# Early access to the gate and up weights, and another order of the first two slabs, in a GFNet and GEGLU kernel

## The chip, the cores and the metric

One NeuronCore of a Trainium2 chip runs the whole kernel. The metric is the time of one execution in microseconds (us) on the device, as the median over runs. Five engines work side by side, each in the order of its own queue: TensorE (PE; its weight loads are shown as PEld), VectorE (DVE), ScalarE (ACT), GpSimd (POOL) and SyncE (SP). They wait for each other through semaphores. 16 DMA engines move data between HBM and the on-chip memory; before the change, all transfers of this kernel are issued by SP.

## The reference

```python
x = A_x                                        # (1, 2048, 640), bfloat16
xn = _layernorm(x, axis=-1)                    # over the 640 columns, eps 1e-5
X = jnp.fft.rfft2(xn.astype(jnp.float32), axes=(-2, -1))
s = irfft2(X * (w_r + 1j * w_i), s=(2048, 640))             # bfloat16
g = silu((gelu(xn @ w_gate) * (xn @ w_up)) @ w_down)        # gelu: tanh form, F = 1536
return x + s * g
```

Two branches start from the same normalized rows: a filter in the frequency domain, and a feed-forward block (FFN) with a gate. Their product is added to the input.

## The kernel before, in words

The 2048 rows are cut into 16 slabs of 128 rows (`X[:, n1, :]`), four slabs to a group. All matmuls, those of the Fourier transforms too, run on TensorE, and the program writes out the order of every engine's queue by hand: a list `back` holds the steps of the FFN (pieces of gate and up for a group, then the down projection), and a table `plan` hangs the other work (statistics, norms, transposes, folds, transforms) on the steps by number, through `put(step, function, arguments)`. For each step the FFN work is issued first and then what `plan` holds for it.

The change lies in the start, up to about 18 us. There:

- `load_x(n0, n)` (L85) and `load_w(k, t0, t1)` (L89) issue the loads on SP: slabs of x, and tiles `t0` to `t1` (128 columns each, for all 640 rows) of the gate (`k = 0`, `Wg`) or up weights (`k = 1`, `Wu`). `load_gu` loads both. Their order is that of the source lines.
- `half_stats(n1, k)` (L183) is the bn_stats instruction of one half of a slab's columns on VectorE; with `k = 1` it is followed by the aggregate (L188), which gives mean and variance (`mva`). `stats` does both halves.
- `root(n0, n)` adds eps on VectorE (`ve`, L197) and raises to the power of -0.5 on GpSimd (`rst`, L199). `norm` (L205) subtracts the mean and multiplies by the root on VectorE; `norm_parts` does it for columns 0 to 383 and 384 to 639 in turn.
- `slab_Tparts(n1)` (L849, L850) transposes a slab on TensorE into a PSUM tile in the same two parts (chunks 0 to 2 and 3 to 4 of 128 columns) and copies each to `xnT`. For slab 0 both copies are ScalarE's; for slab 1 the first is ScalarE's and the second VectorE's. `slab_T` (L531 to L535) does a whole slab.
- `ffn_slab(j, tk)` computes for slab `j` alone, 128 rows wide, the pieces `(t, k)` in `tk`; tiles 0 to 2 are done so for slabs 0 and 1. A piece is five matmuls (L789) into a PSUM bank, two banks for gate (`psg`) and two for up (`psu`). ScalarE then applies gelu to a gate piece (`ge`, L793), and VectorE multiplies the up piece by it into `uT` (L795). `ffn_part(0, t, h)` does the remaining tiles of group 0 for two slabs at a time (256 columns wide), first tiles 3 to 7 of slabs 0 and 1, then tiles 0 to 7 of slabs 2 and 3, which need their norm and transposes.
- `warm_pe(n)` (L590) issues `n` matmuls of 256 columns on a tile of ones, whose results nobody reads.
- `inv_consts` and `inv_rest` compute fourteen columns of constants on VectorE (one element per partition) for the tables of the inverse transform, which `ft_v(5)` and later steps (L353, ScalarE) read. `vt_iota` and `lists` are index ramps on GpSimd.
- ScalarE loads a table of functions when the function to come is not in the one that is loaded (ACT_TABLE_LOAD). The first activation, `warm`, brings gelu's table ahead of its use.

The start as it is issued: loads; constants; statistics and root of slab 0; 19 warming matmuls; norm of slab 0; statistics of slab 1; transposes and copies of slab 0; two warming matmuls; root of slab 1; then the steps of `back`.

Of the kernel before, what the change touches and what calls it, by code (L numbers as in the profile page):

```python
# [10 lines left out]
BF16 = mybir.dt.bfloat16  # L11
# [3 lines left out]
P = 128  # L15
# [62 lines left out]
def build(nc, env):  # L78
# [5 lines left out]
    def load_x(n0, n, eng=nc.sync):  # L84
        eng.dma_start(out=X[:, n0:n0 + n, :], in_=xv[:, n0:n0 + n, :])  # L85

    def load_w(k, t0, t1):
        f0, f1 = t0 * P, t1 * P
        nc.sync.dma_start(out=(Wg, Wu)[k][:, :, f0:f1], in_=(wgv, wuv)[k][:, :, f0:f1])  # L89

    def load_gu(t0, t1):
        for k in range(2):
            load_w(k, t0, t1)

    load_x(0, 1)
    load_w(0, 0, 3)
    load_x(1, 1)
    load_w(1, 0, 1)
    load_w(1, 1, 3)
    load_x(2, 2)  # L100
    load_gu(3, 5)
    load_gu(5, 7)
# [87 lines left out]
    def stats(n1):  # L190
        for k in range(2):
            half_stats(n1, k)

    def root(n0, n):
        m = mva[n0 // 4][:, n0 % 4:n0 % 4 + n, :]
        ve = work.tile([P, 4], FP32, tag="ve", name="ve")[:, 0:n]
        nc.vector.tensor_scalar(out=ve, in0=m[:, :, 1], scalar1=1e-5, scalar2=None, op0=ALU.add)  # L197
        r = work.tile([P, 4], FP32, tag="rst", bufs=4, name="rst")[:, 0:n]
        nc.gpsimd.tensor_tensor(out=r, in0=ve, in1=mhalf[:, 0:n], op=ALU.pow)  # L199
        rall[n0] = r  # L200
        for k in range(n):
            rstd[n0 + k] = r[:, k:k + 1]

    def norm(n1, c0=0, c1_=D):
        nc.vector.tensor_scalar(out=X[:, n1, c0:c1_], in0=X[:, n1, c0:c1_], scalar1=mva[n1 // 4][:, n1 % 4, 0:1],  # L205
                                scalar2=rstd[n1], op0=ALU.subtract, op1=ALU.mult)
        if c1_ == D:
            done.add(("n", n1))
# [3 lines left out]
    negpi = c1("negpi")  # L212
    nc.vector.memset(negpi, -PI_SAFE)
    warm = c1("warm")
    nc.scalar.activation(out=warm, in_=negpi, func=ACT.Gelu_apprx_tanh)
    b_0, b_1 = c1("b_0"), c1("b_1")
    nc.vector.memset(b_0, 320.0)
    nc.vector.memset(b_1, 0.0)
# [99 lines left out]
    fwd_consts()  # L318
    vt_iota(0)
    stats(0)  # L320
    root(0, 1)
    inv_consts()

    def tinv_phase(h):
        sl = slice(8 * h, 8 * h + 8)
# [502 lines left out]
        for t, k in tk:  # L828
            ffn_piece(0, t, k, j * P, j * P + P)

    GG, REST = ((0, 0), (1, 0)), ((0, 1), (2, 0))

    def run(*items):
        for it in items:
# [8 lines left out]
    def slab_Tparts(n1):  # L843
        if n1 == 0:
            xnT[0] = xg.tile([P, 5, 512], BF16, tag="xg", name="xnT0")
        for (a, b), ev in zip(PARTS, (nc.scalar.copy, nc.scalar.copy if n1 == 0 else nc.vector.tensor_copy)):
            pt = psB.tile([P, 5, P], BF16, tag="b")
            for c in range(a, b):
                nc.tensor.transpose(out=pt[:, c, :], in_=X[:, n1, c * P:(c + 1) * P], identity=ident)  # L849
            ev(out=xnT[0][:, a:b, n1 * P:n1 * P + P], in_=pt[:, a:b, :])  # L850
        done.add(("T", n1))

    NP = 8
    back = [(run, (ffn_slab, 0, GG), (norm_parts, 1), (vt_iota, 1), (ffn_slab, 0, REST), (slab_Tparts, 1),
             (ffn_slab, 0, ((1, 1), (2, 1))),
             (half_stats, 2, 0)),
            (run, (ffn_slab, 1, GG + REST[:1]), (half_stats, 2, 1), (root, 2, 1), (ffn_slab, 1, REST[1:])),
            (run, (ffn_slab, 1, ((1, 1), (2, 1))), (norm, 2), (stats, 3), (root, 3, 1))]
    for h in range(2):
        for t in range(0 if h else 3, NP):  # L860
            back.append((ffn_part, 0, t, h))
# [9 lines left out]
    def put(s, *item):  # L871
        plan[s].append(item)

    put(5, norm, 3)
    put(5, slab_T, 2, 1)
    put(6, slab_T, 3, 0)
    for g in range(5):
        put(3 + g, ft_v, g)
        put(8 + g, ft_v, 5 + g)
# [91 lines left out]
            if (n0 + k) % 2 and 1 < (n0 + k + 3) // 2 < 8:  # L971
                put(min(d + (5 + k if n == 3 else 2), vs0 + 41), load_xt, (n0 + k + 3) // 2)

    warm_pe(19)
    norm_parts(0)
    stats(1)
    slab_Tparts(0)
    warm_pe(2)
    root(1, 1)
    inv_rest()  # L980

    put(5, phase_const)

# [35 lines left out]
```

## Time and profile before

| what | us |
|---|---|
| median of 3 runs (lowest, highest) | 201.75 (201.51, 202.1) |
| the profiled execution, its own time | 201.22 |
| its span, first to last instruction | 199.4 |
| TensorE busy | 193.1 (97% of the span) |
| VectorE, ScalarE, GpSimd busy | 131.6, 123.1, 38.0 |
| slab 0 lands (issue 0.72, 2.3 to landing) | 3.05 |
| slab 1 lands (issue 1.65, 3.7 to landing) | 5.35 |
| norm of slab 0, of slab 1 starts | 5.09, 7.63 |
| slab 0's first FFN matmul | 6.59 |
| slab 1's first FFN matmul | 9.01 |

The profile is that of one execution. Times in it count from the start of its span. A line of the timeline gives start, duration, engine, source line, operation, what is written from what, and in brackets how long the engine was idle before it and what ended that. A line of a stretch gives its ends and length, then for TensorE, its weight loads, VectorE, ScalarE and GpSimd the busy time with the number of instructions, then the granted TensorE clock, the DMA engines' share and GB/s. The chain of waits is followed back from the last instruction; each piece has its start, its length and what it is.

### The profile page before, as it was taken

What the parts mean: (1) busy time and instruction counts of PE and PEld (TensorE: products, weight loads), DVE (VectorE), ACT (ScalarE), POOL (GpSimd) and SP (SyncE); (2) the same over time, 40 slices, a digit from 0 to 9 for tenths busy, and PEclk for the clock granted to TensorE, in tenths of its full rate; (3) what the DMA queues carried; (4) which work ended last, traced back from release to release, by engine and by line L of the source; (5) the groups of instructions that cost most, each with busy time, mean ns of one, the idle gap of its engine ahead of it and who ended that gap; (6) DMA issues with size and microseconds to landing.
All of it is one profiled execution on the core that took longest, in us unless ns stands there. A gap on an engine that the chain in (4) does not pass through costs nothing.

```text
span 199.4 us, 4150 instructions
## 1 busy us (share of the span) xinstructions
PE 193.1 (97%) x1534; PEld 118.9 (60%) x1549; DVE 131.6 (66%) x320; ACT 123.1 (62%) x217; POOL 38.0 (19%) x62
## 2 busy tenths in 40 slices
PE   7989999999999999999999999999999999999993
PEld 5778854777555555576633333457765555556772
DVE  7876869999899832223666556423339786878673
ACT  2547657956976677634788687523474747376632
POOL 5427769999030000000000000000000000000000
PEclk9999999999999999999999999999999999999999
DMA  5999999464566647329962022359800416142522
GB/s 176 333 327 337 388 308 186 88 210 173 154 150 158 150 126 278 104 66 298 282 182 98 5 99 102 132 135 292 235 0 35 135 36 194 36 131 46 187 69 66
DMA packets 40325, 32.44 MB, mean 163 GB/s; under 512 B 15088, under 2 KB 38256, under 8 KB 40048
## 3 DMA queue, kind: packets, MB, share of 16 engines
q1 hardware_dynamic: 40304, 32.17, 55.3%
q8 instruction: 12, 0.20, 0.4%
q14 instruction: 9, 0.07, 0.1%
HBM read 19.03 MB, written 7.88 MB: 135 GB/s over the span
## 4 chain that ended last, share of the span: by engine, by line
PE 91%; DVE 4%; DMA 1%; issue 1%; ACT 1%; POOL 1%
PE psu L789 25%; PE psg L789 25%; PE psg L814 13%; PE psu L814 13%; PE pv L706 2%; PE pd L553 2%; PE pu L653 2%; PE pz L543 2%; PE pd L574 2%; PE px L626 2%; DVE st L183 1%; DMA X<-in_A_x_dram 1%; PE pd L557 1%; POOL rst L199 1%; DVE X L205 1%
## 5 line engine op out<-in xcount | busy, mean ns | idle before, releaser
L789 PE MATMUL psu<-xnT,Wu 128*128 128x512 bf16 (+2 forms) x288 | 60.8, 339 | 0.9 <-DVE uT L795 0.3
L789 PE MATMUL psg<-xnT,Wg 128*128 128x512 bf16 (+2 forms) x287 | 60.5, 338 | 0.5 <-issue 0.2
L795 DVE TENSOR_TENSOR uT<-psu,ge 128x512 bf16<-128x512 f32 (+2 forms) x59 | 34.4, 586 | 27.2 <-PE psu L789 21.0
L814 PEld LDWEIGHTS <-uT 128*128 128x128 bf16 x396 | 37.3, 98 | 14.0 <-issue 0.4
L793 ACT ACTIVATE ge<-psg 128x512 bf16<-128x512 f32 (+2 forms) x59 | 30.6, 519 | 22.9 <-PE psg L789 21.1
L789 PEld LDWEIGHTS <-Wu 128*128 128x128 bf16 x295 | 26.9, 98 | 24.7 <-issue 3.2
L789 PEld LDWEIGHTS <-Wg 128*128 128x128 bf16 x295 | 26.6, 98 | 20.6 <-issue 1.6
L814 PE MATMUL psg<-Wd,uT 128*128 128x320 bf16 (+1 forms) x204 | 30.7, 294 | 0.0
L814 PE MATMUL psu<-Wd,uT 128*128 128x320 bf16 (+1 forms) x192 | 28.7, 296 | 0.0
L638 DVE TENSOR_TENSOR X<-xs,W 128x972 bf16<-128x972 bf16 (+2 forms) x22 | 13.3, 648 | 10.2 <-ACT xs L634 9.2
L579 ACT CAST zd<-pd 128x660 bf16<-128x660 f32 x16 | 11.3, 709 | 9.8 <-PE pd L576 6.1
L708 ACT CAST W<-pv 128x640 bf16<-128x640 f32 x16 | 11.1, 696 | 5.0 <-PE pv L706 5.0
L183 DVE BATCH_NORM_STATS2 st<-X 128x6 f32<-128x320 bf16 x32 | 14.0, 477 | 0.3 <-DMA X<-in_A_x_dram 0.3
L731 ACT ACTIVATE W<-pd 128x960 bf16<-128x960 f32 (+2 forms) x14 | 10.1, 780 | 5.6 <-PE pd L557 5.5
L659 ACT CAST X<-pu 128x486 bf16<-128x486 f32 (+4 forms) x22 | 12.3, 558 | 0.3
L634 ACT CAST xs<-px 128x972 bf16<-128x972 f32 (+2 forms) x11 | 10.3, 938 | 2.9 <-PE px L626 2.9
L545 ACT CAST GEN<-pz 128x640 bf16<-128x640 f32 x16 | 11.2, 700 | 1.2 <-PE pz L543 1.2
L823 DVE SCALAR_TENSOR_TENSOR G<-th,psg 128x320 bf16<-128x320 f32 x8 | 3.9, 488 | 12.0 <-ACT th L822 12.0
L737 DVE TENSOR_TENSOR W<-W 128x960 bf16<-128x960 bf16 (+1 forms) x12 | 6.9, 599 | 3.9 <-ACT W L731 3.8
L764 DVE TENSOR_TENSOR Yall<-Yall,G 128x640 bf16<-128x640 bf16 (+3 forms) x19 | 8.3, 435 | 1.6 <-ACT G L819 1.3
L765 DVE TENSOR_TENSOR Yall<-Yall,xt 128x640 bf16<-128x640 bf16 (+3 forms) x19 | 8.3, 439 | 0.7
L199 POOL TENSOR_TENSOR rst<-ve,mhalf 128x1 f32<-128x1 f32 (+1 forms) x7 | 6.0, 854 | 13.8 <-DVE ve L197 13.8
(134 smaller groups left out, 208.3 us busy)
## 6 DMA issues: line engine op xcount, KB each, us to landing
W<-W SPq DMA_DIRECT2D x4, 642.0 KB, 6.0
ZDR<-zd SPq DMA_DIRECT2D x32, 80.2 KB, 2.5
xt<-in_A_x_dram SPq DMA_DIRECT2D x8, 320.0 KB, 3.5
UDR<-X SPq DMA_DIRECT2D x10, 240.8 KB, 2.3
out_dram<-Yall SPq DMA_DIRECT2D x14, 160.0 KB, 2.2
B<-ZDR SPq DMA_DIRECT2D x8, 240.8 KB, 4.3
W<-UDR SPq DMA_DIRECT2D x4, 481.5 KB, 6.8
X<-in_A_x_dram SPq DMA_DIRECT2D x3, 640.0 KB, 6.5
```

The lines of the kernel that those rows point to most:

```text
L183: nc.vector.bn_stats(out=st[:, k, :], in_=X[:, n1, 320 * k:320 * k + 320])
L545: nc.scalar.copy(out=Zt[n1], in_=pz)
L579: nc.scalar.copy(out=zd.rearrange("p c (q e) -> p c q e", e=10), in_=pd[:, :, 0:330].rearrange("p c (e q) -> p c q e", q=33))
L634: nc.scalar.copy(out=xs, in_=px[:, :, 0:n * w].rearrange("p k (h l) -> p k h l", l=w))
L638: nc.vector.tensor_tensor(out=pp[-1], in0=xs, in1=WT[:, :, h0:h0 + n, l0:l0 + w], op=ALU.mult)
L659: nc.scalar.copy(out=us[:, :, :, c0:c0 + (w + 1 - m) // 2], in_=pv[:, :, :, m:w:2])
L708: nc.scalar.copy(out=vs, in_=pv)
L731: nc.scalar.activation(out=eo[:, b, :, a0:a1].rearrange("p k a n -> p a k n"), in_=py[b][:, a0:a1], func=ACT.Copy, scale=(2.0 if silu[a0] ...
L789: nc.tensor.matmul(ps, lhsT=WT[:, c, t * P:(t + 1) * P], rhs=xnT[g][:, c, c0:c1_], start=(c == 0), stop=(c == 4))
L793: nc.scalar.activation(out=ges[t], in_=ps, func=ACT.Gelu_apprx_tanh)
L795: nc.vector.tensor_tensor(out=uT[g][:, t, c0:c1_], in0=ps, in1=ges[t], op=ALU.mult)
L814: nc.tensor.matmul(ph, lhsT=uT[g][:, t, j * P:(j + 1) * P], rhs=Wd[:, t, c0:c1_], start=(t == 0), stop=(t == NT - 1))
```

## The change

Two tiles of 16 partitions and 5 x 2 elements are loaded from the gate and up weights (every eighth row, the first two columns) through ScalarE's queue, ahead of all other work of that engine; nothing reads them. Of the weights, tiles 0 and 1 of the gate come before slab 1, then tiles 0 and 1 of up, then tile 2 of both; before, it was three gate tiles, and up in parts of one and two. Slab 0's root becomes one activation on ScalarE (reciprocal square root of the variance plus eps), the first warm activation brings the table for it, and a second one, right behind the root, brings gelu's. The first half of slab 1's statistics goes ahead of slab 0's norm, the second half behind slab 0's copies. Of slab 0's two copies the first (three chunks) becomes VectorE's. 17 and 4 warming matmuls stand in place of 19 and 2. The pieces of slabs 0 and 1 come in another order, and the statistics of slabs 2 and 3 and the fourteen constants are hung on other steps. An empty step keeps the numbers of the later steps as they were. The computed result is the same.

```diff
+    for k in range(2):
+        corner = consts.tile([NS, 5, 2], BF16, name=f"corner{k}")
+        nc.scalar.dma_start(out=corner, in_=(wgv, wuv)[k][0:P:8, :, 0:2])
     load_x(0, 1)
-    load_w(0, 0, 3)
+    load_w(0, 0, 2)
     load_x(1, 1)
-    load_w(1, 0, 1)
-    load_w(1, 1, 3)
+    load_w(1, 0, 2)
+    load_gu(2, 3)
     load_x(2, 2)
...
+    def root_act(n1):
+        rstd[n1] = c1("rst0")
+        nc.scalar.activation(out=rstd[n1], in_=mva[n1 // 4][:, n1 % 4, 1:2], func=ACT.Abs_reciprocal_sqrt, bias=eps)
+        nc.scalar.activation(out=warm, in_=negpi, func=ACT.Gelu_apprx_tanh)
...
-    nc.scalar.activation(out=warm, in_=negpi, func=ACT.Gelu_apprx_tanh)
+    eps = c1("eps")
+    nc.vector.memset(eps, 1e-5)
+    nc.scalar.activation(out=warm, in_=eps, func=ACT.Abs_reciprocal_sqrt)
...
     stats(0)
-    root(0, 1)
-    inv_consts()
+    root_act(0)
+    half_stats(1, 0)
...
-    GG, REST = ((0, 0), (1, 0)), ((0, 1), (2, 0))
+    GG, UU = ((0, 0), (1, 0), (2, 0)), ((0, 1), (1, 1), (2, 1))
...
-        for (a, b), ev in zip(PARTS, (nc.scalar.copy, nc.scalar.copy if n1 == 0 else nc.vector.tensor_copy)):
+        evs = (nc.scalar.copy, nc.vector.tensor_copy)
+        for (a, b), ev in zip(PARTS, evs[::-1] if n1 == 0 else evs):
...
-    back = [(run, (ffn_slab, 0, GG), (norm_parts, 1), (vt_iota, 1), (ffn_slab, 0, REST), (slab_Tparts, 1),
-             (ffn_slab, 0, ((1, 1), (2, 1))),
-             (half_stats, 2, 0)),
-            (run, (ffn_slab, 1, GG + REST[:1]), (half_stats, 2, 1), (root, 2, 1), (ffn_slab, 1, REST[1:])),
-            (run, (ffn_slab, 1, ((1, 1), (2, 1))), (norm, 2), (stats, 3), (root, 3, 1))]
+    back = [(run, (ffn_slab, 0, GG[:2] + UU[:1]), (norm_parts, 1), (vt_iota, 1), (ffn_slab, 0, UU[1:2] + GG[2:]),
+             (slab_Tparts, 1),
+             (ffn_slab, 0, UU[2:]), (stats, 2), (root, 2, 1)),
+            (run, (ffn_slab, 1, GG + UU[:2]), (norm, 2), (ffn_slab, 1, UU[2:]))]
...
+    back.insert(2, (run,))
+    plan.append([])
+    put(3, half_stats, 3, 0)
+    put(4, half_stats, 3, 1)
+    put(4, root, 3, 1)
+    put(4, slab_T, 2, 1)
     put(5, norm, 3)
-    put(5, slab_T, 2, 1)
     put(6, slab_T, 3, 0)
+    put(5, inv_consts)
+    put(6, inv_rest)
...
-    warm_pe(19)
+    warm_pe(17)
     norm_parts(0)
-    stats(1)
     slab_Tparts(0)
-    warm_pe(2)
+    half_stats(1, 1)
+    warm_pe(4)
     root(1, 1)
-    inv_rest()
```

## The prediction

> **What bounds the kernel now.** I read the page's busy shares first, then the share of the chain of waits by engine, to see which engine sets the end.
>
> ```profile
> PE 193.1 (97%) x1534; PEld 118.9 (60%) x1549; DVE 131.6 (66%) x320; ACT 123.1 (62%) x217; POOL 38.0 (19%) x62
> PE 91%; DVE 4%; DMA 1%; issue 1%; ACT 1%; POOL 1%
> ```
>
> TensorE sets it: 97% busy, 91% of the chain. Only what makes TensorE wait, or start late, can move the time. So I asked for the stretches before and after 17.70 us, where the first half-width gate matmul of the second half of group 0 starts (17.71 in the order of time).
>
> ```profile
> 6.60:17.70 11.10, 10.49 (x126) 9.04 (x124) 8.36 (x33) 6.38 (x19) 4.68 (x9) 1.00 1.11 337
> 17.70:199.40 181.70, 177.33 (x1385) 106.34 (x1398) 118.10 (x245) 114.71 (x197) 30.75 (x44) 1.00 0.52 150
> ```
>
> The change reorders nothing on any engine after about 18 us, and there TensorE runs with no wait over 0.25 us that another engine ends. Whatever is won or lost by 17.71 I carry to the end one for one. Next, the chain in order of time, for the start.
>
> ```profile
> 0.72 2.33 DMA X<-in_A_x_dram
> ...
> 3.07 0.90 DVE st L183 x2
> ...
> 4.24 0.16 DVE ve L197
> ...
> 4.47 0.59 POOL rst L199
> ...
> 5.09 0.64 DVE X L205 x2
> 5.73 0.81 DVE st L183 x2
> ...
> 7.03 0.58 POOL rst L199
> ...
> 7.63 0.39 DVE X L205
> ...
> 10.30 0.23 issue
> 10.53 0.29 DVE uT L795
> ```
>
> The first 17 us are a chain of small steps: slab 0 lands at 3.05 (0.72 + 2.33), its statistics, its root on GpSimd (0.59), its norm at 5.09, then the same for slab 1, whose norm comes at 7.63. Milestones on TensorE, from the timeline: slab 0's first FFN matmul 6.59, with a hole of 0.11 before its fourth (6.70 without the hole); slab 1's transposes 8.07; slab 1's first gate 9.01; tile 3 11.15; the end of the ramp 17.71. Waits in it: 0.25 before 8.07, 0.48 before 10.88, 0.23 before 11.93, 0.31 before 14.41. The 0.48 goes back to VectorE, idle 0.56 before the product at 10.53; I find no operand of it that came so late, so it may belong to its place.
>
> Third, the transfers, since the change moves a statistic to where it needs slab 1 early: the stretches of the load stream (last number GB/s).
>
> ```profile
> 2.40:2.80 0.40, 0.40 (x4) 0.30 (x2) 0.39 (x7) 0.00 (x0) 0.00 (x0) 1.00 0.94 200
> 2.80:3.20 0.40, 0.40 (x4) 0.28 (x2) 0.13 (x1) 0.00 (x0) 0.34 (x1) 1.00 0.45 104
> 3.20:3.60 0.40, 0.40 (x4) 0.28 (x3) 0.40 (x2) 0.00 (x0) 0.40 (x1) 1.00 1.05 330
> 3.60:4.00 0.40, 0.40 (x4) 0.28 (x3) 0.37 (x2) 0.00 (x0) 0.28 (x1) 1.00 1.07 361
> ```
>
> The stream drops to 104 GB/s exactly where the first gate-weight packets follow slab 0. Slab 1, issued at 1.65 and 3.7 to landing, lands at 5.35.
>
> **The change part by part.**
>
> *Small transfers.* Two issues of 160 pieces of 4 bytes in all stand ahead of everything on ScalarE. SP's issues take 0.40 to 0.52 each while its queue is short; two make ScalarE start its table load at 1.65 instead of 0.72, so it ends at 2.9 and the warm activation (0.20) at 3.1, hidden behind slab 0's statistics (to 4.20); without that cover it would cost the 0.9. What they bring is not in the trace. The drop is worth (161 + 257 + 31) x 0.4 us = 180 KB against 361 GB/s, 0.5 us. If it is a cost of the first access to the weights, the small transfers pay it beside slab 0's own start, and slab 1 lands up to 0.5 earlier; if not, 0. They also share the engines with slab 0: ten pieces an engine at the page's mean of 44 ns a packet (55.3% of 16 engines' span over 40304 packets, of some 800 bytes) are 0.4 us at most, and if each engine pays the drop ahead of slab 0 instead, 0.5 us. I take 0.5 earlier, since the drop sits where the first weight packets start and does not come back at the later weights.
>
> *Two gate tiles, not three, before slab 1.* 160 KB less ahead of it: 0.45 at 361 GB/s. Tile 2's gate and up, 256-byte pieces, now land before slabs 2 and 3, which come some 0.3 later less the 0.5; both are wanted only near 9.4. Nothing on the path. Slab 1 then lands at 5.35 - 0.45 - 0.5 = 4.4; filling 2.0 to 2.4 too (232 GB/s) gives 4.26. I take 4.3, bounds 4.0 and 5.5.
>
> *Root on ScalarE, first statistic of slab 1 ahead of slab 0's norm.* Out of the path: the add (0.16 with its hop) and GpSimd's power (0.59). In: one activation on a column, 0.20 (the warm one's time): the root is ready at 4.24 + 0.20 = 4.44, against 5.06. But VectorE takes its queue in order: the statistic of slab 1 waits for 4.3, holds VectorE 0.41 (two take 0.81), and the norm starts at 4.75 instead of 5.09. Of 0.62 won, 0.3 is left. Queued behind it: the norm, and through it the transposes and everything on TensorE.
>
> *The table load that the root brings.* It starts at 4.46 behind the root, 1.28 long, then 0.20: ScalarE is free at 5.96. The copy of chunks 3 and 4, now ScalarE's, is due at 5.95: just covered. The trace shows such a load in use:
>
> ```profile
> 34.21 0.60 ACT L793 ACTIVATE ge<-psg 128x512 bf16<-128x512 f32 x1 [0.75 <-PE psg L789]
> 34.82 1.28 ACT L335 ACT_TABLE_LOAD   x1
> 36.12 0.20 ACT L335 ACTIVATE warm<-negpi 128x1 f32<-128x1 f32 x1
> ```
>
> The Trainium skill, ScalarE: Activation LUTs, "What ACT_TABLE_LOAD costs", counts 1.38 us of draining on top of 1.28 for every switch of set. By that sentence the copy would come at 7.3, TensorE would pass slab 0's first gate at 7.7 instead of 6.87, and the kernel would be slower by about 0.9. The rows show 0.01 us on either side of the load and no drain, so I go by them.
>
> *Copies side by side; 17 and 4 warming matmuls.* The copies took 0.75 one after the other on ScalarE. Now VectorE takes three chunks (between the 0.29 for 256 columns and the 0.48 for 640: 0.36) and ScalarE two, together. Warming matmuls are 0.213 apart before 6.25: four end at 6.5 with transposes from 5.19. Slab 0's FFN goes on without a hole from 6.5, against 6.70: 0.2 won, but slab 1 decides what lasts.
>
> *Slab 1's norm.* Behind slab 0's copy (to 6.05): second statistic 0.48 from 5.98, aggregate, add, power, as at 6.05 to 7.63 before (1.58): norm at 7.56, transposes at 7.99 against 8.07, first gate of slab 1 0.94 later as before: 8.93, 0.08 won. Five of slab 0's six pieces now lie ahead of its transposes; the sixth fits in their copy.
>
> *Slab 1's order.* Three gates first: two banks, so the third waits for the first's gelu (0.46 + 0.28 + hops, 0.80, against 0.56): 0.24. The last up waits for the first's product: 0.26. So 1.68 of matmuls (six pieces of 0.28) and 0.50 is 2.18, against 2.15 before; tile 3 at 11.11 against 11.15.
>
> *Statistics of slab 3 split and later; constants later.* VectorE no longer does two statistics in a row (0.81) ahead of the products, so the waits of 0.23 and 0.31 go. The norm of slab 3 comes later, behind a product whose gelu waits for a copy on ScalarE: 0.27 before slab 3's transposes. Fourteen constants of 0.06 move from time in which VectorE waited for GpSimd to behind that norm, ahead of nothing urgent; without that cover 0.9. Ramp 6.55 - 0.54 + 0.27 = 6.28, end at 17.39: 0.32 won.
>
> *Sum.* 0.32 won with all new waits (0.24 + 0.26 + 0.27 = 0.77) in place; each hangs on two engines within 0.1 to 0.2 of each other, so half may not show: 0.7. I take the middle, 0.5. The profiled execution's 199.4 of span and 1.8 around it are 201.22, 0.5 under the median of 201.75; on the median 201.25.
>
> **The rivals.**
> 1. *Slab 1 earlier still* (landing by 4.0, as if the stream ran at 361 GB/s from its first packet): then the root sets the norm, 4.47, 0.28 earlier, all down the chain: 200.95. For it: 2.0 to 2.4 is slow too. Against it: that slowness is slab 0's own.
> 2. *Slab 1 late, the other side.* The statistic in front of the norm waits for a landing that the small transfers did not hasten or even held up. Each 0.1 later is 0.1 lost; from 4.8 on there is no gain, and at 5.5 it is -0.5 + 1.2 = 0.7 lost: 202.45. For it: nothing in the trace says what the drop is. Against it: 160 KB less are ahead in any case, so 5.35 needs a new cost.
> 3. *TensorE's fast rate comes later.* Its 256-column matmuls are 0.213 apart from 1.17 to 6.25 and 0.109 later. Two fewer come first, and a longer gap before the transposes could put the change off. Slab 0's 30 matmuls at 0.107 in place of 0.056 cost 1.5, less 0.3 of wait at the transposes: about 0.7 over no change: 202.45. Against it: the gap is 0.35 by my sum, no longer than now (5.20 to 5.53).
> 4. *The load drains after all*: 0.9 slower, 202.65.
>
> **How the numbers follow.** Forecast 0.52 (its own range 200.8 to 201.7), rival 1 0.17, rival 2 0.18, rival 3 0.09, rival 4 0.04. A measurement of this kernel tells about 0.3% (0.6 us) from no change. Faster by more: some four tenths of the forecast and nearly all of rival 1, 0.39. Slower: rivals 3 and 4 and most of 2, 0.28. The rest 0.33. The range runs from below rival 1 to the middle of the late cases: 200.6 to 202.4.
>
> **What would show it.** Slab 1's first statistic starting by 4.4 and slab 0's norm by 4.8; no stretch near 100 GB/s at 2.8 to 3.2; ScalarE free of its second load by 6.0; slab 1's transposes near 8.0; the end of the ramp near 17.2. Wrong, if the statistic starts after 4.8, or slab 0's matmuls are still 0.107 apart.

## The result, and the profile after

The changed kernel takes 203.5 us (median of 6 runs, 203.17 to 204.33) against 201.52 for the kernel before on the same chip (6 runs, 201.36 to 202.1): a ratio of 1.0098, with an interval of 1.0076 to 1.0121. It is slower by 2.0 us, where 0.5 faster was forecast, and the time lies 1.1 us above the range. The profiled execution took 203.17 us, its span is 201.4. In all that follows a run over 1.5% above the fastest of its kernel counts in the median and the range, but not in the ratio.

The busy shares and the chain of waits by engine, from the page of the changed kernel:

```profile
PE 194.0 (96%) x1549; PEld 118.3 (59%) x1549; DVE 133.1 (66%) x321; ACT 124.3 (62%) x219; POOL 37.6 (19%) x61
PE 84%; DVE 5%; DMA 4%; ACT 2%; SPq 2%; issue 1%; POOL 1%; DVEq 0%; ACTq 0%
```

TensorE's work is what it was (some matmul records were missing before: 1534 against 1549), but its share of the chain fell from 91% to 84%. VectorE, the transfers and SyncE's queue (SPq) now hold more of it. To see where, I compared the time at which TensorE's n-th weight load starts in the two traces; both programs have the same 1549 of them, counted from 0.

| n-th weight load | before, us | after, us | after minus before |
|---|---|---|---|
| 75 (slab 1) | 9.74 | 10.51 | +0.77 |
| 95 (last pieces of slab 1) | 11.48 | 12.12 | +0.64 |
| 135 (tile 7 of slabs 0 and 1) | 16.11 | 16.22 | +0.11 |
| 145 (behind slab 3's transposes) | 16.94 | 17.72 | +0.78 |
| 185 | 21.33 | 22.82 | +1.49 |
| 600 | 76.34 | 77.84 | +1.50 |
| 680 | 86.17 | 88.30 | +2.13 |
| 1548 | 195.86 | 197.98 | +2.12 |

So the late start of the first two slabs is nearly made good by 16 us. The loss comes in three steps behind it: 0.7 at 17 us, 0.7 at 20 us, 0.6 at 85 us. Its cause has to be looked for at these places.

The chain of waits of the changed kernel in order of time (start, length, what) has the first two of them:

```profile
1.64 3.43 DMA X<-in_A_x_dram
...
5.09 0.49 DVE st L186
5.59 0.29 DVE X L213
...
11.16 0.30 DVE uT L805
...
14.13 0.29 PE pt L541 x5
14.42 0.23 issue
14.65 0.42 DVE uT L805
15.08 0.41 DVE st L186
...
16.00 0.57 POOL rst L202
16.57 0.03 issue
16.59 0.06 DVE X L213
...
18.38 0.66 DVE l_k L276
...
19.42 0.81 DVE o_r L276
20.23 0.33 DVE uT L805
```

Three things are to be seen. Slab 1 lands at 1.64 + 3.43 = 5.07, and its statistic (5.09) stands in front of slab 0's norm. Slab 3's second statistic (15.08) stands behind a product (14.65), so its norm comes at 16.59, against 15.57 before. And two operations on one column of constants, `l_k` and `o_r`, take 0.66 and 0.81 of the chain, where the prediction gave such a column 0.06.

The third step is on ScalarE and TensorE. The timeline rows of the two engines, first of the kernel before and then of the changed one (the bracket gives the idle time ahead of the row and what ended it):

```profile
81.49 0.71 ACT L579 CAST zd<-pd 128x660 bf16<-128x660 f32 x1 [1.61 <-DMA ZDR<-zd]
```

```profile
83.66 0.71 ACT L589 CAST zd<-pd 128x660 bf16<-128x660 f32 x1 [2.28 <-DMA ZDR<-zd]
85.01 0.42 PE L584 MATMUL pd<-FT,GEN 128*128 128x132 bf16 x4 [0.45 <-ACT GEN L555]
```

Before the change, too, ScalarE waits there until a transfer of `ZDR` has freed a `zd` buffer, but TensorE had no wait for it; now the transfer is some 0.7 later and TensorE waits behind ScalarE. The experiments come back to this. A gap of TensorE, here and below, is the time between the starts of two matmuls less the usual spacing of the first; the bracket counts from the matmul's modelled end and comes out some 0.16 lower (0.45 here for a gap of 0.61).

The stretches of the load stream answer the prediction's third view (last number GB/s):

```profile
2.40:2.80 0.40, 0.40 (x4) 0.29 (x2) 0.40 (x7) 0.40 (x1) 0.00 (x0) 1.00 0.85 250
2.80:3.20 0.40, 0.40 (x4) 0.28 (x2) 0.00 (x0) 0.33 (x2) 0.33 (x1) 1.00 0.98 261
3.20:3.60 0.40, 0.40 (x4) 0.27 (x3) 0.32 (x1) 0.00 (x0) 0.40 (x1) 1.00 1.16 300
3.60:4.00 0.40, 0.40 (x4) 0.27 (x3) 0.40 (x2) 0.00 (x0) 0.29 (x1) 1.00 1.17 317
```

The drop to 104 GB/s is gone, as forecast, but the stretches behind it run at 300 and 317 in place of 330 and 361, and slab 1 lands only 0.28 earlier than before.

### The profile page after: what moved, and what is told of

Its sections match the earlier page's. It is cut to its first block, busy times and chain, and to the rows that moved or that the text cites. A ratio compares the mean times of both kernels' runs of the same rounds, so it can differ in the third digit from the quotient of the medians.

```text
span 201.4 us, 4170 instructions
## 1 busy us (share of the span) xinstructions
PE 194.0 (96%) x1549; PEld 118.3 (59%) x1549; DVE 133.1 (66%) x321; ACT 124.3 (62%) x219; POOL 37.6 (19%) x61
## 4 chain that ended last, share of the span: by engine, by line
PE 84%; DVE 5%; DMA 4%; ACT 2%; SPq 2%; issue 1%; POOL 1%; DVEq 0%; ACTq 0%
PE psu L799 23%; PE psg L799 22%; PE psg L824 13%; PE psu L824 13%; PE pv L716 2%; PE pd L563 2%; PE pu L663 2%; DMA ZDR<-zd 2%; PE pd L584 2%; PE px L636 2%; PE pz L553 2%; DMA X<-in_A_x_dram 2%; DVE st L186 1%; SPq L592 1%; DVE uT L805 1%
## 5 line engine op out<-in xcount | busy, mean ns | idle before, releaser
L799 PE MATMUL psg<-xnT,Wg 128*128 128x512 bf16 (+2 forms) x295 | 61.3, 339 | 0.2
L648 DVE TENSOR_TENSOR X<-xs,W 128x972 bf16<-128x972 bf16 (+2 forms) x22 | 13.3, 648 | 10.2 <-ACT xs L644 9.2
L741 ACT ACTIVATE W<-pd 128x960 bf16<-128x960 f32 (+2 forms) x14 | 10.1, 779 | 5.6 <-PE pd L567 5.5
L202 POOL TENSOR_TENSOR rst<-ve,mhalf 128x1 f32<-128x1 f32 (+1 forms) x6 | 5.4, 904 | 16.0 <-DVE ve L200 16.0
```

Of the source, the lines that this page charges most:

```text
L648: nc.vector.tensor_tensor(out=pp[-1], in0=xs, in1=WT[:, :, h0:h0 + n, l0:l0 + w], op=ALU.mult)
L741: nc.scalar.activation(out=eo[:, b, :, a0:a1].rearrange("p k a n -> p a k n"), in_=py[b][:, a0:a1], func=ACT.Copy, scale=(2.0 if silu[a0] ...
L799: nc.tensor.matmul(ps, lhsT=WT[:, c, t * P:(t + 1) * P], rhs=xnT[g][:, c, c0:c1_], start=(c == 0), stop=(c == 4))
```

## The experiments

All ratios are to the kernel before, measured next to each version on the same chip; its median lay between 201.37 and 201.59 each time, so the medians below can be set side by side to about 0.2.

### The three suspected places, one at a time

**The constants put back** to where they were (behind slab 0's root and behind root 1):

```diff
     root_act(0)
+    inv_consts()
     half_stats(1, 0)
...
-    put(5, inv_consts)
-    put(6, inv_rest)
...
     root(1, 1)
+    inv_rest()
```

> The changed kernel with the fourteen constant columns back at the places they had before: the first nine while VectorE waits for slab 1, the last five while it waits for slab 1's root. Theory: in the changed kernel two of the last five ran beside GpSimd's long operations and took 0.74 and 0.81 us instead of 0.15, each ending when a GpSimd operation ended (19.05 and 20.23), and this cost TensorE its waits of 0.50 before 20.62 and 0.24 before 21.95. Then both waits go and the kernel is 0.7 us faster than the changed one, about 202.8. Rival: the two were only late in VectorE's queue and the products behind them would wait anyway; then no more than 0.2 is gained, 203.3.

Measured: 202.37 us (201.55 to 202.66, 5 runs), ratio 1.0034 (1.0004 to 1.0064), against 203.5 with the constants late. From the 165th to the 185th weight load TensorE now needs 2.18, as before the change (2.19), against 2.92 in the changed kernel; `l_k`, `lh` and `l_r`, operations on one column, take 0.15 to 0.16. The second step of the loss is the constants'. But this profile shows something new, taken up below: TensorE's fast rate came 3 us late, and the 95th weight load at 13.27.

**No small transfers:**

```diff
-    for k in range(2):
-        corner = consts.tile([NS, 5, 2], BF16, name=f"corner{k}")
-        nc.scalar.dma_start(out=corner, in_=(wgv, wuv)[k][0:P:8, :, 0:2])
```

> The changed kernel without the small transfers. Theory: they bring slab 1 some 0.2 us or less, since the load stream of the changed kernel runs at 260 to 300 GB/s where it had a drop before, and it is the 512-byte rows that hold it; then slab 1 lands within 0.2 of 5.07 and the time stays within 0.3 of 203.5. Rival: the first access to the weights costs the drop, and without the small transfers slab 1 lands at 5.5 and slab 0's norm, the transposes and the end come 0.4 later, 203.9.

Measured: 204.1 (203.14 to 204.69, 4 runs), 1.0132 (1.0098 to 1.0167). Slab 1's first statistic starts at 4.93, against 5.09 with the small transfers, and slab 0's at 3.03 against 3.28. Over all traces of this study, slab 0 lands between 3.01 and 3.11 in the seven without the small transfers, and between 3.21 and 3.32 in eleven of the thirteen with them (3.08 and 3.11 in the other two), so it lands some 0.2 later for them. Slab 1, with the new order of the weights, lands between 4.91 and 5.61 with them and at 4.74 and 4.91 without: no gain shows, and the spread is too wide for a price. The stretch of 2.80 to 3.20 moves 248 GB/s without them, so it is not they that fill the drop but the other order of the weights. The time of this run says little about them: its profile, too, has the late rate, and it has a larger loss at the constants (3.65 from the 165th to the 185th weight load, against 2.92 in the changed kernel).

**The first statistic of slab 1 behind slab 0's norm:**

```diff
     root_act(0)
-    half_stats(1, 0)
...
     norm_parts(0)
+    half_stats(1, 0)
     slab_Tparts(0)
```

> The changed kernel with the first half of slab 1's statistics behind slab 0's norm, as before the change. Theory: in front of it, it kept the norm from 4.75 to 5.51. Then slab 0's norm starts at 4.8 and its first FFN matmul 0.7 earlier, but slab 1's chain, which sets what follows, wins only what the statistic no longer waits: some 0.1 to 0.4 at slab 1's transposes (8.63), and the end moves by less than that, 203.1 to 203.4. Rival: slab 0's norm is the chain itself, and the end moves by the whole 0.7, 202.8.

Measured: 203.09 (202.61 to 203.37, 4 runs), 1.0084 (1.0069 to 1.01). Slab 0's norm starts at 4.84 in place of 5.50, yet the 95th weight load starts at 12.13, against 12.12 in the changed kernel. The 0.66 won are gone within seven microseconds. The chain of waits of this run, in order of time, says where:

```profile
4.23 5.68 DMA X<-in_A_x_dram
...
9.93 0.90 DVE st L186 x2
...
11.18 0.30 DVE uT L804
...
11.52 0.44 PE psu L798 x5
```

Slab 2 lands at 4.23 + 5.68 = 9.91; its statistics hold VectorE from 9.93, and the product that frees the bank for slab 1's last up piece stands behind them. So in this profile slab 2 sets that piece. But slab 2 landed 0.86 later here than in the changed kernel (9.05), whose own chain runs without a break from slab 1's landing at 5.07 through the statistic, the norms of slab 0 and slab 1 and slab 2's statistics to the last up piece at 11.51. Two versions below have this statistic behind the norm and slab 2 landing at 9.30 and 9.04; in their profiles the piece starts at 11.28 and 10.90 (they have the constants back too, and the second has 19 warming matmuls). So the statistic in front of the norm does seem to cost at the end of the ramp, some 0.2 or more, and the late slab 2 hid that here.

**Slab 3's statistics back** to one block behind slab 1's last up piece:

```diff
-            (run, (ffn_slab, 1, GG + UU[:2]), (norm, 2), (ffn_slab, 1, UU[2:]))]
+            (run, (ffn_slab, 1, GG + UU[:2]), (norm, 2), (ffn_slab, 1, UU[2:]), (stats, 3), (root, 3, 1))]
...
-    put(3, half_stats, 3, 0)
-    put(4, half_stats, 3, 1)
-    put(4, root, 3, 1)
```

> The changed kernel with slab 3's statistics and root where they were before, behind slab 1's last pieces. Theory: in the changed kernel its second half waits behind a product that comes at 14.65, so that slab 3's norm starts at 16.60 instead of 15.57 and TensorE waits 0.67 before slab 3's transposes (17.10). Then that wait goes and the kernel is 0.5 to 0.8 faster than the changed one, 202.7 to 203.0; the constants' waits stay. Rival: the statistics in a row take the time back ahead of the products, as the waits of 0.23 and 0.31 did in the kernel before; then less than 0.2 is gained, 203.4.

Measured: 203.39 (202.1 to 204.92, 9 runs), 1.0081 (1.0047 to 1.0116). Inconclusive by itself: the runs spread over 2.8 us, and the profiled one was the slowest. It was repeated with more warming matmuls, below.

### The parts of the change in the kernel before

**The small transfers alone**, put ahead of the loads of the kernel before (the three lines above, added):

> The kernel before with the small transfers alone added in front of ScalarE's work. Theory: they remove part of the drop to 104 GB/s at 2.8 to 3.2 (slab 1 lands at 5.0 instead of 5.35) at the price of slab 0 landing 0.2 later, as in the changed kernel (3.26 for 3.05); slab 0 is on the chain and slab 1 is not, so the kernel is 0.1 to 0.3 slower than before, 201.7. Rival: the earlier weights and slab 1 are worth more than that, and it is 0.2 faster, 201.3.

Measured: 201.75 (201.15 to 202.32, 8 runs), 1.0019 (0.9997 to 1.004). Slab 0's first statistic moves from 3.07 to 3.26, and all of the start moves with it by 0.2. Slab 1 lands at 5.73, not at the 5.0 expected, and the stretch of 2.80 to 3.20 moves 131 GB/s: the drop stays.

**The constants alone**, moved to steps 5 and 6 in the kernel before:

> The kernel before with only the fourteen constant columns at the later steps that the change gives them. Theory: VectorE operations on these columns that come while GpSimd runs a long operation are held until it ends (in the changed kernel two of them, 0.74 and 0.81 us for 0.15). Here GpSimd's long pair runs from about 16.3 to 18.7, so one or two of the last five columns show 0.5 to 1.2 us and end within 0.03 of the end of a GpSimd operation, TensorE waits behind the product that follows, and the kernel is 0.3 to 1.0 us slower than before, 201.7 to 202.4. Rival: the long times in the changed kernel came from the operands or from the crowded queue; then no operation is over 0.2 us and the kernel is within 0.2 of before.

Measured: 201.92 (201.67 to 202.9, 10 runs), 1.0026 (1.0008 to 1.0045). In the profile, that of the slowest run, three operations on one column take 0.44, 1.07 and 0.61, and TensorE has a gap of 0.93 before 20.31, where it waits for a product behind them. In the median the loss is 0.4, so it differs from run to run.

**Slab 0's root on ScalarE and the swapped copies**, in the kernel before, without the rest:

```diff
-    root(0, 1)
+    root_act(0)
     inv_consts()
...
     norm_parts(0)
-    stats(1)
     slab_Tparts(0)
     warm_pe(2)
+    stats(1)
```

> The kernel before with slab 0's root on ScalarE, the two copies swapped between the engines and slab 1's statistics behind slab 0's copies; no small transfers, weights in the old order. Theory: with nothing in front of it, slab 0's norm follows the root, at 4.55 instead of 5.09, the second table load ends about 5.75 and is covered, and slab 0's matmuls start at 6.4 or earlier; slab 1's chain starts 0.15 later behind the copy and sets the rest: within 0.3 of before, 201.1 to 201.7. Rival: slab 0 leads the whole ramp, and 0.4 is won, 201.0.

Measured: 201.24 (200.94 to 202.22, 10 runs), 0.9999 (0.998 to 1.0017). Slab 0's norm comes at 4.68 and its first FFN matmul at 5.90, 0.7 earlier than before; at the 145th weight load 0.21 is left of it (16.73 against 16.94), and in the time nothing that can be told from no change.

### All three put back

**The changed kernel with the constants, slab 3's statistics and slab 1's first statistic put back** (the three diffs above together):

> The changed kernel with three parts undone: the constants and slab 3's statistics at their old places, and slab 1's first statistic behind slab 0's norm. What stays of the change: the small transfers, the order of the weights, the root and the second copy on ScalarE, the order of the pieces. Theory: the three parts hold all of the loss, 0.7 for the constants, 0.6 for slab 3, and the statistic's part behind them; then it is even with the kernel before or up to 0.4 faster, 201.0 to 201.5, where TensorE's fast rate sets in at 6.3, and about 1 us slower in executions where it sets in at 9.4, as in the profile of the first experiment. Rival: the start of the changed kernel has a loss of its own, in the order of slab 1's pieces (third gate waiting for the first's gelu, last up for the first product); then 201.8 to 202.2.

Measured: 201.65 (200.87 to 203.98, 10 runs), 1.0012 (0.9981 to 1.0042). The 2.0 us are gone. What stays of the change in this version (small transfers, order of the weights, root on ScalarE, copies side by side, the order of the pieces, slab 2's statistics) is together worth no measurable time. The 145th weight load is at 17.07, the 185th at 21.44, against 16.94 and 21.33 before. Set against the profile of the changed kernel, 0.2 of the 2.0 is won up to the 135th weight load, 0.4 at slab 3's transposes, 0.7 at the constants and 0.6 near 85 us.

### TensorE's rate

Two profiles above, and that of slab 3's statistics put back, show the small matmuls of slab 0 at half speed. Rows of TensorE in the changed kernel, and then in the version with the constants back:

```profile
6.74 0.74 PE L799 MATMUL psg<-xnT,Wg 128*128 128x128 bf16 x10
7.31 0.72 PE L799 MATMUL psu<-xnT,Wu 128*128 128x128 bf16 x10
```

```profile
7.22 1.27 PE L800 MATMUL psg<-xnT,Wg 128*128 128x128 bf16 x10
8.29 1.27 PE L800 MATMUL psu<-xnT,Wu 128*128 128x128 bf16 x10
```

Ten matmuls of 128 columns take 0.57 from one row to the next in the first and 1.07 in the second. In the profiles of this study the spacing halves at a time between 4.0 and 6.7 us, or else between 9.3 and 10.2 (three profiles, all of programs in which TensorE stands idle for 1.0 to 1.1 us from 4.8 on), and nowhere between. The later onset costs 1.15 at the 95th weight load (13.27 against 12.12 in the changed kernel). The Trainium skill, TensorE: Matmul & The Clock Gate, "Part 1: The HAM clock gate", says that the rate is judged in stretches of 3.4 us which run on whatever the kernel does. The three late onsets (9.3, 9.6, 10.1) less that length give 5.9 to 6.7, which are ends of stretches that hold the idle time, so the rows agree if such a stretch doesn't count. The next run takes the idle time away.

**22 warming matmuls in place of 17** in the changed kernel, beside the changed kernel itself:

```diff
-    warm_pe(17)
+    warm_pe(22)
```

> The changed kernel with 22 warming matmuls ahead of slab 0's transposes instead of 17, so that TensorE has no idle stretch of 1.1 us between 4.8 and 5.9. Theory (the onset of the fast rate is judged in fixed stretches of some 3.4 us whose phase is free from run to run; a stretch that holds the 1.1 us of idle time doesn't count, and the onset then comes a stretch later, at 9.3 to 10.1 as seen in three profiles): now every stretch from 1.2 on is busy, so the onset comes by 8.0 in every run; the upper group of times (204 and more) goes, the median falls to 202.6 to 203.2, and nothing else changes: the held VectorE operations near 18.3 and 19.4 and the wait of 0.67 before tile transposes of slab 3 stay. Rival (the spread of the times comes from transfers, not from TensorE's rate): the same spread as the changed kernel in the same call, median within 0.2 of it.

> The changed kernel itself once more, as the measure for the others on the same chip: 203.2 to 204.4, median 203.4 by both theories; by the theory of the free phase its times fall in two groups some 1 us apart.

Measured: 203.56 (203.28 to 203.9, 5 runs), 1.0096 (1.0079 to 1.0113), against 204.2 (203.7 to 204.54, 4 runs), 1.0135 (1.0114 to 1.0155). The upper group is gone and the median is 0.64 lower, as the theory had it, though the median lies 0.4 above the top of what was expected. But the two profiles, both with the early rate, differ by 0.42 at the end, of which 0.34 come near 85 us; so the rival, that the spread comes from the transfers, isn't excluded. With four and five runs, and no profile of a run of the changed kernel itself with the late onset, this agrees with the theory and doesn't prove it.

**Slab 3's statistics back, with 22 warming matmuls:**

> The changed kernel with slab 3's statistics where they were and 22 warming matmuls. Against the changed kernel with 22 warming matmuls this is slab 3's statistics alone, with TensorE's rate out of it. Theory (the late statistic makes the norm of slab 3 late by 1.0 and TensorE wait 0.67 at its transposes, of which 0.24 stays): 0.4 to 1.0 faster than that, median 202.0 to 202.5; the VectorE operations held at 18 to 20 stay, since the constants stay late. Rival (the late norm is recovered by the end of the ramp): no difference.

Measured: 203.19 (202.42 to 203.86, 6 runs), 1.0076 (1.0054 to 1.0098): 0.37 less than with the statistics late. The row of slab 3's transposes, first with the statistics late and then with them back, shows the wait that the theory named:

```profile
17.02 0.45 PE L541 MATMUL pt<-ident,X 128*128 128x128 bf16 x5 [0.51 <-DVE X L213]
```

```profile
16.96 0.45 PE L541 MATMUL pt<-ident,X 128*128 128x128 bf16 x5
```

TensorE's gap ahead of it is 0.67 in the first and 0.25 in the second. The median came out 0.7 higher than expected. The difference of 0.37 is close to the 0.42 of the two gaps, but the intervals of the two ratios overlap, and in the two profiles only 0.12 is left at the end, since the second one was 0.36 late already at the 75th weight load. So the wait is shown, and what it is worth in time is not.

**The mended version with 19 warming matmuls:**

> The version with constants, slab 3's statistics and slab 1's first statistic put back behind the norm, and 19 warming matmuls instead of 17 (idle stretch 0.1 instead of 0.5). Theory: the runs at 203.9 go, all runs lie at 200.9 to 202.1, median 201.3; about 0.1 to 0.2 below the kernel before at best. Rival: the runs at 203.9 come from transfers and stay, 2 in 10.

Measured: 202.36 (201.32 to 203.52, 12 runs), 1.0042 (1.002 to 1.0063). A miss on both counts: the spread stayed, and the median came out 0.7 higher than with 17 (their intervals overlap). Its profile has a good ramp and then loses it at one place. This version has two warming matmuls more than the kernel before, so that its 147th and 602nd weight loads are the other's 145th and 600th: they start at 16.69 and 76.07, 0.25 and 0.27 ahead of the kernel before. (The 0.5 to 0.7 in two of the expectations below leave out this shift.) The place of the loss:

```profile
82.28 0.71 ACT L589 CAST zd<-pd 128x660 bf16<-128x660 f32 x1 [2.67 <-DMA ZDR<-zd]
83.63 0.42 PE L584 MATMUL pd<-FT,GEN 128*128 128x132 bf16 x4 [0.84 <-ACT GEN L555]
```

### The train of transfers near 80 us

In the traces of the kernel before, of the changed one and of the mended ones, SyncE issues transfers without a pause of more than 0.5 us from 46 to 48 us on to between 81 and 86: `ZDR`, transposed transfers, loads of the second half of `W` and two copies within `W` of 642 KB. TensorE's gap near 84 us, behind ScalarE's wait for one of them, is under 0.1 in the kernel before, 0.61 in the changed one, 1.0 in the mended one with 19 warming matmuls, and 1.33 in the slowest run of slab 3's statistics put back. The loss doesn't follow the ramp: from the 600th to the 680th weight load the changed kernel loses 0.63 at a shift of 1.50 against the kernel before, the version with slab 1's first statistic behind the norm 0.08 at the same shift, and the mended one with 19 warming matmuls 1.0 although it is 0.27 ahead. Four runs have these two copies, and two like them near 43 us, issued by GpSimd, which is idle ahead of 80 us:

```diff
-        nc.sync.dma_start(out=v[2 + pm:P:4], in_=v[pm:P:4])
+        nc.gpsimd.dma_start(out=v[2 + pm:P:4], in_=v[pm:P:4])
```

in the mended version with 19 warming matmuls, the kernel before, the changed kernel, and the mended version without the small transfers:

> The mended version with 19 warming matmuls, and the two 642 KB transfers within W issued by GpSimd, idle there for 25 us, instead of SyncE. Theory (SyncE's train of issues from 46 to 86 us is full, and its transfers of ZDR end up behind the two large ones, so that whatever the first 18 us win is taken back near 84 us): the wait of 1.0 near 83.6 goes, the profile keeps its 0.5 to 0.7 against the kernel before to the end, median 200.7 to 201.1, few runs over 202. Rival (the wait comes from the bytes of the large transfers, whoever issues them): the wait stays at 0.5 to 1.3, median 202.

> The kernel before with the same edit. Theory: its train leaves it some 0.2 of room (no wait over 0.2 near 84 us in its profile), so no change: 201.3 to 201.7. Rival: the train costs it something too, 201.0 or less.

> The changed kernel with the same edit. Theory: its wait of 0.4 to 0.6 near 85 us goes, its other losses stay: 203.0 to 203.5 against 203.5 to 204.2 for the changed kernel. Rival: no change.

> The first of these four without the small transfers ahead of slab 0. Theory (they make slab 0 land 0.2 later and slab 1 no earlier, as the kernel before showed when it was given them): 0.1 to 0.2 faster than the first, 200.6 to 200.9. Rival (they help the weights): slower than the first by 0.2 or more.

Measured: 203.59 (203.05 to 206.87, 6 runs), 1.012 (1.0081 to 1.016); 203.37 (202.52 to 203.71, 6 runs), 1.009 (1.007 to 1.011); 205.43 (204.8 to 210.29, 5 runs), 1.0189 (1.0169 to 1.0209); 203.49 (202.26 to 208.3, 6 runs), 1.0071 (1.0044 to 1.0097). A miss: every one is slower than without the edit. The copies of the second half now start at 70.7 to 73.3 instead of 73.4 to 75.1, run beside SyncE's transposed transfers, and the longest of these takes 2.6 to 3.7 us to issue in place of 1.3; TensorE's gap before 82.3 grows to 2.07 in the kernel before. So taking these issues off SyncE wins nothing. It may be the copies themselves that cost, beside what else is under way, but the edit also changed their queue and their start, so that isn't shown. And the kernel before has next to no room there: when something delays the train, it pays at once. The share of the small transfers can't be read under so large a wait.

So ten transfers were taken out of the train altogether, in the mended version with 19 warming matmuls and in the kernel before; they are issued 15 to 19 steps earlier:

```diff
-    ... (32, 32, 35, 35, 38, 38, 41, 41, 47, 48))):
+    ... (16, 17, 18, 19, 20, 21, 22, 23, 32, 33))):
```

> The mended version with 19 warming matmuls, with the eight loads of the second half of W 16 to 18 steps earlier (some 22 to 36 us instead of 48 to 66) and its two copies of 642 KB some 48 us instead of 75. Theory (the train takes the gain): SyncE is idle again between ZDR transfers from about 55 us on, TensorE waits under 0.3 near 84 us in all runs, and the 0.5 to 0.7 that the profile had at 75 us reaches the end: median 200.6 to 201.0, highest under 202. Rival (the ramp's gain is lost for another reason, or the early loads cost the ramp as much): 201.5 or more.

> The kernel before with the same ten transfers earlier. Theory: its profile has no wait for the train, so at most its outlying runs go: median 201.1 to 201.5. Rival (early loads hurt the ramp): 202 or more; then the run above is read against this one.

Measured: 206.42 (204.41 to 208.72, 6 runs), 1.0221 (1.0185 to 1.0257), and 202.78 (202.4 to 202.89, 6 runs), 1.0062 (1.0045 to 1.008). Rows of the second, the kernel before with early loads:

```profile
44.05 0.38 PE L543 MATMUL pz<-Tfwd,f 128*128 128x128 bf16 x4 [1.17 <-DMA Tfwd<-Tinv]
...
79.09 0.71 ACT L579 CAST zd<-pd 128x660 bf16<-128x660 f32 x1 [0.79 <-PE pd L576]
81.83 0.71 ACT L579 CAST zd<-pd 128x660 bf16<-128x660 f32 x1 [0.79 <-PE pd L576]
84.58 0.71 ACT L579 CAST zd<-pd 128x660 bf16<-128x660 f32 x1 [0.79 <-PE pd L576]
```

Near 80 us the theory holds in both: the casts come every 2.74 us, wait for TensorE and no longer for `ZDR`, and TensorE's gap there is 0.19. That gap is one that the kernel before has too, at 84.77. But the early loads push the first of the transfers `Tfwd<-Tinv` on SyncE from 37.39 to 40.54 in the kernel before; it lands at 43.92, its first reader starts at 44.05, and TensorE's gap there is 1.34. In the mended version a gap of 3.98 stands at the same matmuls, before 46.48, and the same transfer is late: it is issued at 43.83 and lands at 46.35, against 38.20 and 40.66 without the early loads, and the reader follows 0.13 behind it, as in the kernel before with early loads. The trace puts this wait down to VectorE, and the chain behind it to a row of eight operations of GpSimd; but these, and VectorE's, come within 0.15 of their times without the early loads, so the transfer is what fits. Behind this gap the granted clock is 0.50 from 45.70 to 49.10, and the 602nd weight load starts 5.1 later than without the early loads. The wait went to another place, and it was larger there. No version run here beats the kernel before by more than the noise.

## Why the prediction was wrong, point by point

Of the signs that the prediction named, the drop at 2.8 to 3.2 went as forecast. But slab 1's first statistic started at 5.09 (4.4 forecast, and over 4.8 named as the sign of being wrong), slab 0's norm at 5.50 (4.8), slab 1's transposes at 8.63 (8.0), and the ramp ended at 18.48 (17.2).

**"The change reorders nothing on any engine after about 18 us ... Whatever is won or lost by 17.71 I carry to the end one for one."** Wrong twice. The constants were moved to just that place and cost TensorE 0.72 between 18 and 22. And near 85 us the changed kernel lost 0.6 more, at ScalarE's wait for a transfer, and the mended version with 19 warming matmuls lost 1.0 after winning 0.27. What delays the train in one profile and not in another is open; the shift of the ramp alone doesn't.

**Constants: "fourteen constants of 0.06 move ... behind that norm, ahead of nothing urgent; without that cover 0.9."** The step that failed most plainly: the size of one operation was taken from a place where GpSimd had no long operation. Rows of VectorE and then of GpSimd in the changed kernel:

```profile
18.30 0.74 DVE L276 SCALAR_TENSOR_TENSOR l_k<-pb,l_s 128x1 f32<-128x1 f32 x1
18.97 0.15 DVE L288 SCALAR_TENSOR_TENSOR lh<-hk,pb 128x1 f32<-128x1 f32 x1
19.15 0.16 DVE L276 SCALAR_TENSOR_TENSOR l_r<-lh,l_k 128x1 f32<-128x1 f32 x1
19.34 0.15 DVE L265 TENSOR_SCALAR i_r<-l_r 128x1 f32<-128x1 f32 x1
19.42 0.81 DVE L276 SCALAR_TENSOR_TENSOR o_r<-l_r,cq 128x1 f32<-128x1 f32 x1
```

```profile
17.85 2.38 POOL L336 TENSOR_SCALAR GEN<-GEN,u,ph_t 128x1024 int32<-128x1024 int32 x2 [1.29 <-DVE ph_t L276]
```

GpSimd's row holds two operations, which end at 19.04 and 20.22; VectorE's two long ones end at 19.04 and 20.23. An operation on one column thus waited until GpSimd's was over. The same ends within 0.01 are seen in the runs with 22 warming matmuls, with the constants late in the kernel before, and in the changed kernel's repetition. There `l_r`, which escaped above, was held too (1.07 to 1.08), and TensorE's gap in the repetition was 1.23 instead of 0.50, so the loss differs from run to run. In all nine traces with the constants late `l_r` starts 0.12 behind GpSimd's second operation by the record; in six it is held and in three it isn't, and what decides it is open. Behind the constants stands a product that TensorE waits for, which the prediction took for nothing urgent. The Trainium skill, SBUF — State Buffer, "Who interferes with whom", states that a VectorE operation with two inputs in SBUF contends with a GpSimd operation that reads SBUF, and the later one waits to the end. The rows agree: `l_k`, `l_r` and `o_r` have two inputs, `i_r` has one and was not held in any of them. The 0.16 of `l_r` in three traces it doesn't explain. Read beforehand, it would have spoken against this step.

**Statistics of slab 3: "0.27 before slab 3's transposes."** That the norm comes late behind a product was right, the term mis-sized: 0.67 is what it measured, 0.25 with the statistics in their old place. The prediction saw the norm behind a product; it was the second statistic that stood behind one (14.65), and that product's gelu waited in turn. The waits of 0.23 and 0.31 went, as forecast, and brought back 0.53 of the 0.64 by which the 95th weight load was late; the 0.67 took that away again.

**Small transfers: "I take 0.5 earlier."** Wrong: no gain shows. With them slab 1 lands at 4.91 to 5.61, without them at 4.74 and 4.91, and slab 0 lands 0.2 later for them. The drop at 2.8 to 3.2 went without them (248 GB/s) and stayed with them alone (131), so it is not a cost of a first access that they pay.

**Two gate tiles: "160 KB less ahead of it: 0.45."** Right in size, as far as single profiles tell: without the small transfers slab 1's statistic starts at 4.93, 0.4 before the old landing of 5.35 (5.26 to 5.80 in the other profiles of the old order without small transfers). That is 0.63 later than the sum's 4.3, of which 0.5 are the small transfers' forecast.

**Root on ScalarE: "the root is ready at 4.44", norm at 4.75.** The activation took 0.29, not the 0.20 of the warm one, and the statistic in front waited for slab 1: norm at 5.50. Rival 2 named this wait and its place, and priced it at 0.1 lost for each 0.1. The chain of the changed kernel does run through it, to slab 1's last piece at 11.51, but the price comes out smaller: with the norm 0.66 earlier slab 1's transposes came 0.28 earlier, and in that profile a late slab 2 took even this. Of what the root alone wins in the kernel before, 0.7 at slab 0's first matmul, 0.21 is left at the end of the ramp.

**The table load: ScalarE "free at 5.96".** Right within the 0.3 by which all was later: 1.28 from 4.76, then the warm activation at 6.05 with nothing between. The drain of rival 4, for which the prediction cited the Trainium skill, ScalarE: Activation LUTs, does not show here either; the copy at 6.50 waited for its transposes.

**Slab 1's order: waits of 0.24 and 0.26.** Measured 0.25 and 0.34. Right.

**Rival 3, the fast rate later, 0.09.** It happens, in three of the profiles of programs with 17 warming matmuls, at a cost of 1.15 at slab 1's last pieces. The profile of the changed kernel doesn't have it. The sum that set it aside took the idle stretch as 0.35; it is 1.1, because the norm is late.

So the sum failed in two terms: 0.5 for the small transfers, which win nothing, so that slab 0's norm waits for slab 1, and nothing for the constants, which cost 0.7. It mis-sized a third (slab 3, 0.67 for 0.27), and it carried the ramp to the end one for one, where 0.6 more was lost near 85 us.

## What to carry to other kernels

When a small operation is moved, look at what the other engines run at its new place, not only at what stands behind it in its own queue: here columns of 0.06 took up to 1.08 beside GpSimd's long operations. A gain at the start counts only up to the next landing or queue that doesn't move with it; look for those (slab 2, which landed anywhere from 8.20 to 9.91 us, and a train of transfers near 80) before summing what the first engine wins. And be wary of an idle stretch in the warming of TensorE: of the six profiles in which 17 warming matmuls left one of 1.0 to 1.3 us, three had the fast rate some 3 us late. When two traces are compared by the number of a matmul, count the matmuls that were added ahead of it.

## What the runs showed of the hardware that was not expected

- A VectorE operation on a single column took 0.44 to 1.08 us in place of 0.06 to 0.16, ending within 0.01 of a running GpSimd operation, and each of these had two column inputs; one with a single one between them took 0.15.
- TensorE's change from 107 to 56 ns per matmul of 128 columns came between 4.0 and 6.7 us or between 9.3 and 10.2, from run to run.
- From 2.8 to 3.2 us the load stream moved 35 to 131 GB/s with three gate tiles ahead of slab 1 (six traces) and 173 to 275 with two (14 traces), with and without the small transfers. Why is open.
- Behind a gap of 3.98 us on TensorE the granted clock was 0.50 for 3.4 us.
- Open, too, is what spreads the runs of the mended versions by 2 to 3 us (200.87 to 203.98): the rate and the wait near 84 us were each seen in single profiles, but no profile of their slowest runs was taken.
